# Loading the first four blocks of a linear-attention kernel as two spans of 256 tokens, two tokens per partition, and running them on quarter tiles

## The chip, the cores and the metric

One core of one Trainium2 chip. The metric is the device time of one execution in microseconds (us), from the first to the last event on the core. The profile's own span is some 2 us shorter than this time. The median of the kernel before was 227.73 us when the prediction was made (3 runs, 227.59 to 228.28).

## The reference

Linear attention with a decay per head over 4 sequences of 768 tokens, 8 heads of 64, then a feed-forward part with a gate `h * cos(h)` over all 3,072 tokens. Inputs and output are float32.

```
for b in range(nb):                       # blocks of 64 tokens, in order
    intra = einsum('bhic,bhjc->bhij', qb, kb) * Dmask
    intra = einsum('bhij,bhjd->bhid', intra, vb)
    inter = einsum('bhid,bhde->bhie', qb * lam_pow, kv_state)
    out[:, :, sl] = intra + inter
    kv_state = lam_block * kv_state + einsum('bhsd,bhse->bhde', kb_dec, vb)
...
x = out.transpose(0, 2, 1, 3).reshape(3072, 512)
h = x @ w_in                              # 512 -> 2048
return (h * cos(h)) @ w_out               # 2048 -> 512
```

## The kernel before

The kernel works on blocks of 128 tokens, 24 in all, and on 7 feed-forward tiles of 2 or 4 blocks. A small planner in the program puts all tasks in order for each engine. Some words that come back: the lead-in is the time until the first feed-forward matmul; a hidden matmul is one with `w_in`, a projection one with `w_out`; scores are the products of q and k, masked ones those after the mask; an eviction copies a finished product out of PSUM, where TensorE's rows write (the `ps_` tiles); the granted clock is the share of its full clock that TensorE was given. The parts that matter here are the loads of a block (q, k and v, each token of each head a run of 256 bytes), the chain of loads and weights, and the dummy matmuls of the lead-in.

```
def add_load(n, prio, deps=()):
    b, s0 = n // NB, (n % NB) * P
    for j, (name, src) in enumerate((("q_f", q), ("k_f", k), ("v_f", v))):
        def emit(name=name, src=src):
            t = loads.tile([P, H, D], F32, tag=name, name=name)
            i = nc.sync.dma_start(out=t, in_=src[b, :, s0:s0 + P, :].transpose([1, 0, 2]))
            # ... waits for every d in deps
...
if n >= DMA_FROM:          # from block 8 on: q and k transposed by DMA, on the queue of the loads
    first_out, T[n] = dma("SP", 1.2, 1.3, transposes_dma, n - LAG + 1.5, [a, b], get="qkT", ordered=False)
...
# ORDER = "b0 b1 b2 b3 i0 i1 i2 i3 o0 o1 o2 o3": four blocks, w_in in quarters, w_out in quarters
for at, name in enumerate(names):
    which, n = name[0], int(name[1:])
    deps = [kept[-4 if which != "b" else -2]] if at and (names[at - 1][0] == "b") != (which == "b") else []
    # weights wait for block 2's v, block 4's loads for the third quarter of w_out
...
def keep_awake(us, at, cols):            # dummies on TensorE until the first feed-forward matmul
    for _ in range(int(us / (cols / (1200.0 if at < 5.0 else 2400.0) + 0.0025))):
        nc.tensor.matmul(idle_ps[:, :cols], lhsT=ident, rhs=ident[:, :cols], start=True, stop=True)
```

## Time and profile before

| | before |
|---|---|
| time, median | 227.73 us |
| span of the profiled run, granted clock of TensorE | 226.4 us, 0.992 |
| TensorE busy | 208.4 us, 92% |
| VectorE busy | 118.6 us, 52% |
| first feed-forward matmul | 23.03 us |
| block 4's first load leaves | 38.36 us |

TensorE is the bound, so what can be won are its waits; the prediction below shows where they are. Two views are needed to follow what comes later. The first is the queue of SyncE in the timeline (start, duration, engine, line, operation), here the last load of the lead-in, block 4's first load, and the transpose of block 9, for which TensorE waits at 72.61:

```profile
14.12 0.81 SPq L201 DMA_DIRECT2D v_f<-in_v_dram  x1
...
38.36 0.37 SPq L201 DMA_DIRECT2D q_f<-in_q_dram  x1
...
66.22 2.62 SPq L271 DMA_TRANSPOSE qkT<-qk  x1
```

The second is the table of stretches: the stretch and its length, then busy us (and instructions) of TensorE, of its weight loads, of VectorE, ScalarE and GpSimd, then the granted clock, the share of DMA time and GB/s:

```profile
4.00:8.00 4.00, 1.61 (x21) 1.29 (x19) 1.32 (x3) 3.63 (x6) 0.51 (x1) 1.00 1.27 231
8.00:12.00 4.00, 4.00 (x69) 3.36 (x66) 1.82 (x4) 1.35 (x3) 2.54 (x3) 1.00 1.34 220
```

While only block loads move, the DMA share is above 1, and 231 and 220 GB/s move.

### The profile page before, as it was taken

How to read it: one execution, taken by the hardware profiler on the slowest of the kernel's cores; microseconds unless marked ns; L12 is line 12 of the kernel's file. 1: busy time of each engine (PE TensorE's matmuls, PEld its weight loads, DVE VectorE, ACT ScalarE, POOL GpSimd, SP SyncE). 2: the span in 40 equal slices, each digit the busy share in tenths (PEclk: the TensorE clock that was granted, in tenths of full speed). 3: DMA queues.
4: the chain of work that ended last, by engine and by line, in shares of the span. 5: the costliest groups of instructions: out<-in, count | busy, mean ns of one | idle time of the engine just before them, and what ended most of it. 6: DMA issues, size and time to landing. Idle time of an engine off the chain costs nothing.

```text
span 226.4 us, 4556 instructions
## 1 busy us (share of the span) xinstructions
PE 208.4 (92%) x1806; PEld 113.7 (50%) x1832; DVE 118.6 (52%) x210; ACT 105.4 (47%) x179; POOL 67.4 (30%) x84
## 2 busy tenths in 40 slices
PE   4899998599984999999999999999999999999993
PEld 4778443255663554454545444554545444565541
DVE  1455486047755477778766537746646343432310
ACT  5455675112462455745544454454454544544420
POOL 2469300378543474544354104412000000000000
PEclk9999999999999799999999999999999999999999
DMA  5999999999999999999999985723011001111112
GB/s 122 222 199 163 179 204 206 227 203 258 229 247 227 209 226 195 240 230 189 252 170 262 185 190 101 151 76 84 10 49 46 14 35 46 46 46 49 46 46 93
DMA packets 99764, 33.85 MB, mean 149 GB/s; under 512 B 92448, under 2 KB 96800, under 8 KB 99744
## 3 DMA queue, kind: packets, MB, share of 16 engines
q1 hardware_dynamic: 95376, 29.24, 63.0%
q0 software_dynamic: 4224, 4.19, 11.5%
q8 instruction: 14, 0.23, 0.4%
q10 hardware_dynamic: 144, 0.13, 0.2%
q14 instruction: 6, 0.05, 0.1%
HBM read 27.27 MB, written 6.29 MB: 148 GB/s over the span
## 4 chain that ended last, share of the span: by engine, by line
PE 84%; DMA 7%; ACT 4%; issue 2%; DVE 2%; POOL 0%; POOLq 0%
PE ps_h L393 35%; PE ps_f L431 33%; PE ps_s L295 4%; DMA qkT<-qk 3%; PE ps_o L320 3%; PE ps_o L324 2%; PE ps_h L489 2%; PE ps_f L393 2%; DMA q_f<-in_q_dram 2%; PE ps_t L265 2%; DMA lam_bc<-in_lam_dram 1%; PE ps_kv L308 1%; DMA out_dram<-o_sb 1%; DVE g L406 1%; ACT cos L400 1%
## 5 line engine op out<-in xcount | busy, mean ns | idle before, releaser
L400 ACT ACTIVATE cos<-ps_h,halfpi 128x512 f32<-128x512 f32 (+1 forms) x107 | 66.2, 624 | 77.3 <-PE ps_h L393 77.2
L406 DVE TENSOR_TENSOR g<-ps_h,cos 128x512 bf16<-128x512 f32 (+1 forms) x107 | 65.0, 610 | 69.9 <-ACT cos L400 69.2
L431 PE MATMUL ps_f<-w_out_sb,g 128*128 128x512 bf16 x349 | 90.6, 382 | 3.6 <-issue 1.4
L393 PE MATMUL ps_h<-xT,w_in_sb 128*128 128x512 bf16 (+1 forms) x421 | 92.5, 350 | 0.9 <-DVE g L406 0.6
L393 PEld LDWEIGHTS <-w_in_sb 128*128 128x128 bf16 x448 | 43.5, 99 | 44.0 <-issue 2.0
L431 PEld LDWEIGHTS <-g 128*128 128x128 bf16 x384 | 36.5, 98 | 41.3 <-issue 2.6
L239 POOL TENSOR_TENSOR qk<-q_f,q_scale 128x512 bf16<-128x512 f32 x23 | 24.0, 1044 | 60.3 <-DMA q_f<-in_q_dram 25.2
L302 DVE TENSOR_TENSOR s_m<-ps_s,mask 128x512 bf16<-128x512 f32 x48 | 31.2, 685 | 7.7 <-PE ps_s L295 6.3
L247 POOL TENSOR_TENSOR v_s<-v_f,v_scale 128x512 bf16<-128x512 f32 x24 | 25.1, 1044 | 24.1 <-DMA v_f<-in_v_dram 16.0
L444 ACT COPY o_sb<-ps_f 128x512 f32<-128x512 f32 x23 | 13.5, 587 | 23.8 <-PE ps_f L431 23.6
L330 ACT CAST xT<-ps_o 128x512 bf16<-128x512 f32 x24 | 13.9, 580 | 3.9 <-PE ps_o L324 3.8
L314 DVE CAST kv_bd<-ps_kv 64x256 bf16<-64x256 f32 x32 | 13.4, 418 | 2.9 <-PE ps_kv L308 2.4
L489 PE MATMUL ps_h<-ident 128*128 128x64 bf16 x232 | 12.0, 213 | 1.6 <-POOL ident masks.py:199 1.6
L295 PE MATMUL ps_s<-qkT 64*128 64x128 bf16 x192 | 9.7, 222 | 3.5 <-DMA qkT<-qk 2.8
L243 POOL CAST qk<-k_f 128x512 bf16<-128x512 f32 x20 | 12.2, 611 | 1.9 <-DMA k_f<-in_k_dram 1.7
L268 DVE COPY qkT<-ps_t 128x512 bf16<-128x512 bf16 (+1 forms) x12 | 6.1, 513 | 12.4 <-PE ps_t L265 12.2
L489 PEld LDWEIGHTS <-ident 128*128 128x128 bf16 x232 | 10.2, 111 | 2.4 <-POOL ident masks.py:199 1.6
L265 PE MATMUL ps_t<-ident,qk 128*128 128x128 bf16 x64 | 6.6, 236 | 4.4 <-DVE qk L239 2.0
L324 PE MATMUL ps_o<-s_m,v_s 128*64 128x128 bf16 x192 | 9.6, 220 | 0.0
L320 PEld LDWEIGHTS <-kv_bd 128*64 128x64 bf16 x160 | 5.1, 109 | 7.0 <-issue 5.9
L320 PE MATMUL ps_o<-qkT,kv_bd 128*64 128x128 bf16 x160 | 8.3, 225 | 0.0
L295 PEld LDWEIGHTS <-qkT 64*128 64x128 bf16 x192 | 5.5, 95 | 5.3 <-DMA qkT<-qk 3.0
(34 smaller groups left out, 58.1 us busy)
## 6 DMA issues: line engine op xcount, KB each, us to landing
q_f<-in_q_dram SPq DMA_DIRECT2D x24, 256.0 KB, 4.3
k_f<-in_k_dram SPq DMA_DIRECT2D x24, 256.0 KB, 4.7
v_f<-in_v_dram SPq DMA_DIRECT2D x24, 256.0 KB, 4.8
out_dram<-o_sb SPq DMA_DIRECT2D x23, 256.0 KB, 2.2
w_in_sb<-in_moe_w_in_dram POOLq DMA_DIRECT2D x4, 512.0 KB, 7.4
w_out_sb<-in_moe_w_out_dram POOLq DMA_DIRECT2D x4, 512.0 KB, 14.3
qkT<-qk SPq DMA_TRANSPOSE x16, 4.2
out_dram<-o_sb SPq DMA_DIRECT2D x1, 128.0 KB, 1.7
```

Source lines behind the costliest of these rows:

```text
L239: (nc.vector if n == 0 else nc.gpsimd).tensor_mul(live["qk", n][:, 0], live.pop(("q_f", n)), q_scale[:, c, :].unsqueeze(2).to_broadcast([P ...
L247: nc.gpsimd.tensor_mul(live["v_s", n], live.pop(("v_f", n)), v_scale[:, c, :].unsqueeze(2).to_broadcast([P, H, D]))
L295: nc.tensor.matmul(t[:, i, p, :], lhsT=live["qkT", n][h, 1, p, :], rhs=live["qkT", n][h, 0, p, :], start=True, stop=True)
L302: nc.vector.tensor_mul(live["s_m", n][:, i], live["s", n][:, i], mask.unsqueeze(1).to_broadcast([P, NP, P]))
L320: nc.tensor.matmul(t[h, p, :], lhsT=kv_bd[(n - 1) % NK][:, p, h], rhs=live["qkT", n][:, 0, p, :], start=(p == 0), stop=False, skip_group_c ...
L324: nc.tensor.matmul(t[h, p, :], lhsT=live["v_s", n][:, 2 * p + i, :], rhs=live["s_m", n][:, i, p, :], start=(p == 0 and c == 0), stop=True, ...
L330: nc.scalar.copy(live["xT", i][:, :, j * P:(j + 1) * P], live.pop(("o", n)))
L393: ins = nc.tensor.matmul(t[:, :cols], lhsT=w_in_sb[:, kd, f * P:(f + 1) * P], rhs=live["xT", i][:, kd, :cols], start=(kd == 0), stop=(kd = ...
L400: nc.scalar.activation(c[:, :cols], live["h", i, f][:, :cols], AF.Sin, bias=halfpi)
L406: nc.vector.tensor_mul(live["g", i][:, f, :cols], live.pop(("h", i, f))[:, :cols], live.pop(("c", i, f))[:, :cols])
L431: nc.tensor.matmul(live["f", i, j], lhsT=live["g", i][:, f, j * P:(j + 1) * P], rhs=w_out_sb[:, f, :], start=(f == 0), stop=(f == KF - 1))
L489: nc.tensor.matmul(idle_ps[:, :cols], lhsT=ident, rhs=ident[:, :cols], start=True, stop=True)
```

## The change

The intent is to shorten the lead-in. Blocks 0 to 3 become two spans of 256 tokens. Partition u holds the tokens 2u and 2u+1, which lie next to each other in memory, so a run is 512 bytes. Scores and values are then computed on 64x64 quarters of the array (64*64 in TensorE's rows), for even and odd tokens apart, with a mask that knows the order of tokens. The weights wait for k of span 1 in place of block 2's v. Their order relative to block 4's load does not change: the latter still waits for the third quarter of w_out.

```diff
-ORDER = "b0 b1 b2 b3 i0 i1 i2 i3 o0 o1 o2 o3"
+ORDER = "i0 i1 i2 i3 o0 o1 o2 o3"
+    def add_span_load(name, src, x, prio):
+        def emit():
+            t = live[name, "sp", x] = consts.tile([P, H, 2, D], F32, name=f"{name}_sp{x}")
+            return start_load(t.rearrange("u h s d -> u h (s d)"),
+                              src[0, :, 2 * P * x:2 * P * (x + 1), :].rearrange("h (u s) d -> u h (s d)", s=2), ())
+        _, load_t[name, "sp", x] = dma("SP", 1.8, 0.5, emit, prio)
...
+        def scores(hp):                       # in add_span; values() is built the same way
+            for p in range(2):
+                for s in range(2):
+                    for rows, _ in chunks:
+                        for i, h in enumerate(halves):
+                            nc.tensor.matmul(L["s", hp][i][rows, p, s, :], lhsT=L["kT"][h, s, 2 * hp + p, rows],
+                                             rhs=L["qT"][h, :, 2 * hp + p, rows], ...)
...
+                if n0 + j < 2 * SPANS:        # a block of a span is stored in two halves
+                    for s, h in enumerate(halves):
+                        nc.sync.dma_start(out=out[r0 + s:r0 + P:2, cols], in_=live["o_sb", i, j][h, cols])
+                    return
...
+    for j, (name, x) in enumerate((("q", 0), ("k", 0), ("q", 1), ("k", 1), ("v", 0), ("v", 1))):
+        add_span_load(name + "_f", {"q": q, "k": k, "v": v}[name], x, -20 + j)
+        kept.append(load_t[name + "_f", "sp", x])
+    hold = kept[-3]
-        deps = [kept[-4 if which != "b" else -2]] if at and ...
+        deps = [kept[-2]] if at and ...
-            keep_awake((t.start - now) * (0.95 if now < 2.0 else 0.6), now, D)
+            keep_awake((t.start - now) * (0.95 if now < 2.0 else 0.75), now, D)
```

Not in this excerpt: the scaling, transposes and evictions of the spans, shared between VectorE, ScalarE and GpSimd; a third buffer for the state; the planner's start times for the set-up work.

More of the change, by code (lines that the diff above doesn't have):

```diff
@@ L16 @@
 DMA_FROM = 8
+SPANS = 2
 LAG = 2
@@ L35 @@
 class Planner:
-    LAT = {"PE": 0.2, "ACT": 0.06, "DVE": 0.08, "POOL": 0.1, "SP": 0.0, "DMA": 0.0}
+    LAT = {"PE": 0.2, "ACT": 0.06, "DVE": 0.08, "POOL": 0.1, "SP": 0.0, "DMA": 0.0, "SETUP": 0.0}
+    SETUP = {"POOL": 5.6, "DVE": 5.6, "ACT": 7.5, "SP": 1.3}
     def __init__(self, bufs):
@@ L49, in order @@
     def order(self):
-        free, done = {}, []
+        free, done = dict(self.SETUP), []
         got = {tag: [] for tag in self.bufs}
@@ L137 @@
     make_identity(nc, ident)
+    pos_sp = consts.tile([P, SPANS, 2], F32)
+    nc.gpsimd.iota(pos_sp, pattern=[[2 * P, SPANS], [1, 2]], base=-S // 2, channel_multiplier=2,
+                   allow_small_or_imprecise_dtypes=True)
+    mask_sp = consts.tile([P, 2, P], F32)
+    nc.gpsimd.memset(mask_sp, 1.0)
+    for i in range(2):
+        m = mask_sp[i * D:(i + 1) * D].rearrange("u k (s t) -> u k s t", s=2)
+        nc.gpsimd.affine_select(out=m, in_=m, compare_op=ALU.is_ge, fill=0.0,
+                                base=0, pattern=[[-1, 2], [1, 2], [2, D]], channel_multiplier=-2)
     mask = consts.tile([P, P], F32)
@@ L143 @@
     nc.vector.memset(halfpi, math.pi / 2.0)
-    NK = 2
+    NK = 3
     kv_bd = [consts.tile([P, NP, P], BF16, name=f"kv_bd{i}") for i in range(NK)]
@@ L149 @@
     nc.scalar.activation(lnl, lam_bc, AF.Ln)
+    expo_sp = consts.tile([P, SPANS, H, 2], F32)
+    nc.vector.tensor_mul(expo_sp, pos_sp.unsqueeze(2).to_broadcast([P, SPANS, H, 2]),
+                         lnl.unsqueeze(1).unsqueeze(3).to_broadcast([P, SPANS, H, 2]))
+    q_sp = consts.tile([P, SPANS, H, 2], F32)
+    nc.scalar.activation(q_sp, expo_sp, AF.Exp)
     expo = consts.tile([P, NB, H], F32)
@@ L152 @@
                          lnl.unsqueeze(1).to_broadcast([P, NB, H]))
+    v_sp = consts.tile([P, SPANS, H, 2], F32)
+    nc.scalar.activation(v_sp, expo_sp, AF.Exp, scale=-1.0)
     q_scale = consts.tile([P, NB, H], F32)
@@ L194, in dma, with start_load @@
         return t, d
+    def start_load(o, x, deps):
+        i = nc.sync.dma_start(out=o, in_=x)
+        for d in deps:
+            tc.add_manual_dep(i.ins, getattr(d, "issue", d).ins.ins.name, mybir.DependencyInfo(
+                mybir.DependencyClass.Sync, mybir.DependencyReason.DATA), reason="order of loads")
+        return i
+    def add_span_load(name, src, x, prio):
[4 more added lines that the diff above has]
+        _, load_t[name, "sp", x] = dma("SP", 1.8, 0.5, emit, prio)
     def add_load(n, prio, deps=()):
@@ L200, in emit @@
                 t = loads.tile([P, H, D], F32, tag=name, name=name)
-                i = nc.sync.dma_start(out=t, in_=src[b, :, s0:s0 + P, :].transpose([1, 0, 2]))
-                for d in deps:
-                    tc.add_manual_dep(i.ins, getattr(d, "issue", d).ins.ins.name, mybir.DependencyInfo(
-                        mybir.DependencyClass.Sync, mybir.DependencyReason.DATA), reason="order of loads")
                 live[name, n] = t
-                return i
+                return start_load(t, src[b, :, s0:s0 + P, :].transpose([1, 0, 2]), deps)
             issue, load_t[name, n] = dma("SP", 1.2, 0.45, emit, prio + 0.1 * j, deps, get=name)
@@ L227 @@
     T, Sc, So, V, Vo, U, Uo = ({} for _ in range(7))
-    parts = {}
+    parts, Uo_sp = {}, {}
+    chunks = [(halves[c], c) for c in range(2)]
     def add_attention(n):
@@ L379, in add_attention, with add_span, prep, prep_k @@
             parts[n] = finish
+    def add_span(x):
+        pa = lambda part: -1000.0 + 2 * x + part
+        pv = lambda part: -990.0 + 2 * x + part
+        cut = [slice(4 * hp, 4 * hp + 4) for hp in range(2)]
+        us = {"DVE": 0.69, "POOL": 1.1}
+        vec = {"DVE": nc.vector, "POOL": nc.gpsimd}
+        L = {name: consts.tile([P, 2, H, D], BF16, name=f"{name}_sp{x}") for name in ("q", "k", "v")}
+        L.update({name: consts.tile([P, 2, NP, P], BF16, name=f"{name}_sp{x}") for name in ("qT", "kT")})
+        L["s_m"] = consts.tile([P, 2, NP, 2, P], BF16, name=f"s_m_sp{x}")
+        place = lambda t, hp: t[:, :, cut[hp]].rearrange("u s h d -> u h s d")
+        def prep(name, hp, e):
+            vec[e].tensor_mul(place(L[name], hp), live[name + "_f", "sp", x][:, cut[hp]],
+                              (q_sp if name == "q" else v_sp)[:, x, cut[hp]].unsqueeze(3).to_broadcast([P, 4, 2, D]))
+        def prep_k(hp):
+            nc.scalar.copy(place(L["k"], hp), live["k_f", "sp", x][:, cut[hp]])
+        def transposes(name, hp):
+            t = L["t", name, hp] = bank(("ps_t", "ps_f")[hp], [P, 2, 2, P], BF16)
+            for s in range(2):
+                for p in range(2):
+                    h = 4 * hp + 2 * p
+                    nc.tensor.transpose(t[:, s, p, :], L[name[0]][:, s, h:h + 2, :], ident)
+        def transposes_out(name, hp, e):
+            (nc.scalar.copy if e == "ACT" else nc.vector.tensor_copy)(L[name][:, :, 2 * hp:2 * hp + 2, :], L["t", name, hp])
+        def scores_bank():
+            L["s", 1] = [bank("ps_t" if x else "ps_o", [P, 2, 2, P], F32)]
+        def scores(hp):
+            if x and hp:
+                L["s", 1].append(bank("ps_f", [P, 2, 2, P], F32))
+            elif hp:
+                live["spare"] = bank("ps_h", [P, NP, P], F32)
+                L["s", 1].append(live["spare"].rearrange("u (p s) t -> u p s t", p=2))
+            else:
+                t = bank("ps_s", [P, 2, 2, 2, P], F32)
+                L["s", hp] = [t[:, 0], t[:, 1]]
+            for p in range(2):
+                for s in range(2):
+                    for rows, _ in chunks:
+                        for i, h in enumerate(halves):
+                            nc.tensor.matmul(L["s", hp][i][rows, p, s, :], lhsT=L["kT"][h, s, 2 * hp + p, rows],
+                                             rhs=L["qT"][h, :, 2 * hp + p, rows],
+                                             start=True, stop=True, skip_group_check=True)
+        def scores_out(hp, i):
+            nc.vector.tensor_mul(L["s_m"][:, i, 2 * hp:2 * hp + 2], L["s", hp][i],
+                                 mask_sp.unsqueeze(1).to_broadcast([P, 2, 2, P]))
+        def update(rows, n):
+            for p in range(NP):
+                for s in range(2):
+                    for i, h in enumerate(halves):
+                        nc.tensor.matmul(kv_ps[h, p, :], lhsT=L["k"][rows, s, 2 * p + i, :], rhs=L["v"][rows, s, 2 * p + i, :],
+                                         start=(n == 0 and p == 0 and s == 0), stop=True, skip_group_check=True)
+        def update_out(n, h, e):
+            (nc.scalar.copy if e == "ACT" else nc.vector.tensor_copy)(kv_bd[n % NK][h, :, h], kv_ps[h])
+        def values_bank():
+            if not x:
+                L["o"] = [bank("ps_o", [P, NP, P], F32), live["spare"]]
+        def values():
+            if x:
+                t = bank("ps_s", [P, 2, NP, P], F32)
+                L["o"] = [t[:, 0], t[:, 1]]
+            for p in range(NP):
+                for s in range(2):
+                    for rows, c in chunks:
+                        for i, h in enumerate(halves):
+                            nc.tensor.matmul(L["o"][c][h, p, :], lhsT=L["v"][rows, s, 2 * p + i, :],
+                                             rhs=L["s_m"][rows, i, p, s, :],
+                                             start=(p == 0 and s == 0), stop=True, skip_group_check=True)
+        def carried(c):
+            for p in range(NP):
+                nc.tensor.matmul(L["o"][c][:, p, :].rearrange("e (s u) -> e s u", s=2),
+                                 lhsT=kv_bd[(2 * x + c - 1) % NK][:, p, :], rhs=L["qT"][:, :, p, chunks[c][0]],
+                                 start=False, stop=True, skip_group_check=True)
+        def values_out(c, e, pairs):
+            if ("xT", 0) not in live:
+                live["xT", 0] = work.tile([P, KD, 4 * P], BF16, tag="xT", name="xT")
+            n = 2 * x + c
+            (nc.scalar.copy if e == "ACT" else nc.vector.tensor_copy)(
+                live["xT", 0][:, pairs, n * P:(n + 1) * P], L["o"][c][:, pairs])
+        so, kt, v_t = [], [], []
+        for hp in range(2):
+            e = "DVE" if hp == 0 else "POOL"
+            a = pl.add(e, us[e], [load_t["q_f", "sp", x]], partial(prep, "q", hp, e), pa(-0.9 + 0.1 * hp))
+            kt.append(pl.add("ACT", 0.61, [load_t["k_f", "sp", x]], partial(prep_k, hp), pa(-0.9 + 0.1 * hp)))
+            e = "DVE" if hp == 0 else "POOL"
+            v_t.append(pl.add(e, us[e], [load_t["v_f", "sp", x]], partial(prep, "v", hp, e), pa(-0.7 + 0.1 * hp)))
+            outs = []
+            for name, src in (("qT", a), ("kT", kt[hp])):
+                e = "ACT" if x else "DVE"
+                t = pl.add("PE", MM(P, 4), [src], partial(transposes, name, hp), pa(-0.5 + 0.1 * hp), get=("ps_t", "ps_f")[hp])
+                outs.append(pl.add(e, 0.58 if e == "ACT" else 0.42, [t], partial(transposes_out, name, hp, e), pa(-0.5 + 0.1 * hp)))
+                t.frees = [outs[-1]]
+            if hp:
+                s0 = pl.add("PE", 0.0, outs, scores_bank, pa(0.1 + 0.1 * hp), get="ps_t" if x else "ps_o")
+                s1 = pl.add("PE", MM(P, 8) + 0.2, [s0], partial(scores, hp), pa(0.1 + 0.1 * hp), get="ps_f" if x else None)
+            else:
+                s0 = None
+                s1 = pl.add("PE", MM(P, 8) + 0.2, outs, partial(scores, hp), pa(0.1 + 0.1 * hp), get="ps_s")
+            two = [pl.add("DVE", 0.69, [s1], partial(scores_out, hp, i), pa(0.1 + 0.1 * hp + 0.05 * i)) for i in range(2)]
+            s1.frees = two
+            if s0:
+                s0.frees = two
+            so += two
+        c0, c1 = 2 * x, 2 * x + 1
+        out_of = {}
+        def add_update(c):
+            n = 2 * x + c
+            U[n] = pl.add("PE", MM(D, 16) + 0.2, v_t + kt + Uo_sp.get(n - 1, []), partial(update, chunks[c][0], n), n - 1100.0 if n < 3 else -900.0)
+            Uo_sp[n] = [pl.add(e, 0.4, [U[n]] + ([V[n - NK + 1]] if n > NK - 1 else []), partial(update_out, n, h, e), n - 1100.0 if n < 3 else -900.0)
+                        for h, e in zip(halves, ("ACT", "DVE"))]
+        add_update(0)
+        v0 = pl.add("PE", 0.0, so + v_t, values_bank, pv(0.2), get=None if x else "ps_o")
+        v1 = pl.add("PE", MM(P, 8) + 0.2, [v0], values, pv(0.2), get="ps_s" if x else None)
+        first_out = pl.add("PE", MM(P, 4), [v1] + Uo_sp[c0 - 1], partial(carried, 0), pv(0.25)) if x else v1
+        second = pl.add("PE", MM(P, 4), [v1] + Uo_sp[c0], partial(carried, 1), pv(0.3))
+        V[c0], V[c1] = first_out, second
+        Vo[c0] = pl.add("ACT", 0.6, [first_out], partial(values_out, 0, "ACT", slice(0, NP)), pv(0.3))
+        ends = [pl.add(e, 0.4, [second], partial(values_out, 1, e, p), pv(0.35))
+                for e, p in (("DVE", slice(0, 2)), ("ACT", slice(2, NP)))]
+        v0.frees = v1.frees = [Vo[c0]] + ends
+        Vo[c1] = pl.add("SETUP", 0.0, ends, None, 0.0, lat=0.15)
+        add_update(1)
+        Uo[c1] = pl.add("SETUP", 0.0, Uo_sp[c1], None, 0.0, lat=0.1)
@@ L464, in add_ffn @@
             evacs[0].frees = stores
+    kept = []
+    for j, (name, x) in enumerate((("q", 0), ("k", 0), ("q", 1), ("k", 1), ("v", 0), ("v", 1))):
+        add_span_load(name + "_f", {"q": q, "k": k, "v": v}[name], x, -20 + j)
+        kept.append(load_t[name + "_f", "sp", x])
     names = ORDER.split()
-    names += [f"b{n}" for n in range(NBLK) if f"b{n}" not in names]
-    kept = []
+    names += [f"b{n}" for n in range(2 * SPANS, NBLK) if f"b{n}" not in names]
+    hold = kept[-3]
     for at, name in enumerate(names):
         which, n = name[0], int(name[1:])
-        deps = [kept[-4 if which != "b" else -2]] if at and (names[at - 1][0] == "b") != (which == "b") else []
+        deps = [kept[-2]] if at and (names[at - 1][0] == "b") != (which == "b") else []
         if which == "b":
@@ L478 @@
         hold = deps[0] if deps else (None if which == "b" else hold)
+    for x in range(SPANS):
+        add_span(x)
     for i in range(len(TILES)):
-        for n in range(first[i] + (i > 0), min(first[i + 1] + 1, NBLK)):
+        for n in range(max(2 * SPANS, first[i] + (i > 0)), min(first[i + 1] + 1, NBLK)):
             add_attention(n)
```

## The prediction

> **What bounds the kernel now.** I read the page first, then the timeline of the lead-in, the timeline of TensorE alone, and the busy time by stretches. The page says that TensorE is busy 92% of the span, so only its waits can be won back:
>
> ```profile
> span 226.4 us, 4556 instructions
> PE 208.4 (92%) x1806; PEld 113.7 (50%) x1832; DVE 118.6 (52%) x210; ACT 105.4 (47%) x179; POOL 67.4 (30%) x84
> PEclk9999999999999799999999999999999999999999
> ```
>
> Part of this busy time is line 489, dummy matmuls[...] while the first four blocks come in. So the lead-in must be read from its own timeline:
>
> ```profile
> 7.49 1.04 POOL L247 TENSOR_TENSOR v_s<-v_f,v_scale 128x512 bf16<-128x512 f32 x1 [5.42 <-DMA v_f<-in_v_dram]
> 11.03 1.04 POOL L247 TENSOR_TENSOR v_s<-v_f,v_scale 128x512 bf16<-128x512 f32 x1 [1.38 <-DMA v_f<-in_v_dram]
> 15.29 1.04 POOL L247 TENSOR_TENSOR v_s<-v_f,v_scale 128x512 bf16<-128x512 f32 x1 [2.04 <-DMA v_f<-in_v_dram]
> 16.28 0.94 POOL L216 DMA_DIRECT2D w_in_sb<-in_moe_w_in_dram  x1
> ...
> 22.39 0.59 ACT L330 CAST xT<-ps_o 128x512 bf16<-128x512 f32 x1 [0.70 <-PE ps_o L324]
> ...
> 23.03 1.89 PE L393 MATMUL ps_h<-xT,w_in_sb 128*128 128x512 bf16 x7
> ```
>
> The third load of each block lands at 7.49, 11.03 and 15.29 us: 3.90 us per block of 768 KB (786,432 bytes), or 202 GB/s. The lead-in is paced by these loads, the weights' first transfer waits for them until 16.28, and the useful work of the feed-forward part starts at 23.03.
>
> TensorE's own timeline shows two later stalls:
>
> ```profile
> 37.64 2.75 PE L431 MATMUL ps_f<-w_out_sb,g 128*128 128x512 bf16 x12 [0.64 <-DVE g L406]
> 40.89 1.02 PE L431 MATMUL ps_f<-w_out_sb,g 128*128 128x512 bf16 x4 [0.50 <-DMA w_out_sb<-in_moe_w_out_dram]
> 43.87 0.40 PE L265 MATMUL ps_t<-ident,qk 128*128 128x128 bf16 x4 [1.96 <-POOL qk L239]
> ...
> 72.61 0.40 PE L295 MATMUL ps_s<-qkT 64*128 64x128 bf16 x8 [2.85 <-DMA qkT<-qk]
> ```
>
> The first is 0.64 + 0.50 + 1.96 = 3.10 us. Behind the 1.96 stands a DMA: block 4's q load is issued only at 38.36, when the third quarter of the output weights has landed. The second is 2.85 us for a DMA transpose, and costs more than it shows, as the stretch after it ran at 0.53 of the clock:
>
> ```profile
> 33.00:37.00 4.00, 3.95 (x18) 1.70 (x18) 3.14 (x6) 3.16 (x5) 0.00 (x0) 1.00 1.24 207
> ...
> 73.00:76.00 3.00, 3.00 (x14) 1.64 (x13) 2.12 (x4) 0.95 (x2) 2.23 (x3) 0.53 1.02 187
> 76.00:80.00 4.00, 3.74 (x46) 2.20 (x46) 1.27 (x4) 2.06 (x4) 0.77 (x2) 0.93 1.14 218
> ```
>
> Lost clock: 3.00 x 0.47 + 4.00 x 0.07 = 1.7 us. The rest of the span is TensorE at work, apart from a tail of some 6 us that the change doesn't touch. The last two figures of a row are the DMA share and GB/s: 207 while only weights move, counted in bf16 although float32 is read, so about 400 GB/s of reads. The same engines thus read twice as fast in 2 KB runs as in the 256 bytes of a block load's descriptors.
>
> [...] the trace has 0.69 us for each masked 128x512 eviction, while eight matmuls take 0.40. [...]
>
> **The change part by part.**
>
> Loads. Twelve loads of 1,024 descriptors of 256 bytes become six of 1,024 with 512 bytes. One load took 1.30 us. At unchanged time per descriptor a span load takes 1.3 us[...]. I take 1.7 (308 GB/s)[...], as the weights show the engines can read at 400. The first q load of before was in by about 5.0, so q0, k0, q1, k1, v0, v1 land at about 5.4, 7.1, 8.8, 10.5, 12.2, 13.9, against some 19 for before's last.
>
> Compute of the lead-in. It does not shrink with the loads. VectorE of before: one scaling 0.69, eight transpose copies 0.43, eight masked scores 0.645 = 9.3 us. After, from the program's order: four scalings 2.76, four copies 1.7, eight masked scores 5.2, four state halves at 0.43 = 1.7, two output halves at 0.42 = 0.8: 12.2 us. It starts at 5.5 (the scale's activation ends there), so cannot end before 17.7. By hand, engine by engine in program order:
> - ScalarE is free for k at about 7.4 (two more small activations than before); k halves at 8.0 and 8.6; VectorE has the first kT at about 9.4, scales q1 until 10.1, second kT 10.5.
> - Masked scores of span 0 until 13.2, v0's scaling 13.9; ScalarE's transposes of span 1 give scores at 14.2, masked by 15.6.
> - Then a strict chain of states, each update waiting for the eviction before it, halves one after the other on ScalarE and VectorE: about 16.3, 18.4, 20.0. Span 1's second scores and v1's scaling fill VectorE between.
> - Carried product 20.3, then three evictions in a row, 0.6 + 0.42 + 0.38: 21.7. With some overlap that I could not settle, 20.3 to 21.7; I take **21.0, a gain of 2.0 us**. Quarter tiles add 64 small matmuls to scores and values[...] in place of dummies: nothing.
>
> Weights. Their first transfer now waits for k1 (10.5), not for block 2's v (15.29, issued 16.28). From there v0 and v1 have still some 3.4 us of traffic, the weights 4.19 MB / 0.205 = 20.5 us. Last landing: 9.2 + 3.4 + 20.5 + 1.5 (latency) = 34.6, third quarter 2.5 earlier, about **32.1 against 38.36: 6 us earlier**.
>
> First stall. Hidden matmuls take 14.0 us: 35.0; wait for the last gate 0.64; sixteen projections 3.46: 39.1. Block 4's loads leave at 32.1, its q lands 4.25 later, scaling and k's copy 1.75: 38.1. So the waits of 0.50 and 1.96 both go: **2.46 us**; I count 2.2.
>
> Second stall. The transpose is issued behind 21 loads and four stores from block 4 on, and before, stores ready at 42.5 left only at 51.79: that queue is paced by the DMA, not by TensorE. It comes some 6 us earlier, less about 0.5 for stores split in two; TensorE only 4.2. So the 2.85 shrinks by about 1.3, and with a shorter pause part of the lost clock comes back. I count **1.8 of 4.5 us**.
>
> Against: the planner has reordered everything after, which I put at 0.3. Sum 2.0 + 2.2 + 1.8 - 0.3 = 5.7: 227.7 - 5.7 = **222.0 us**.
>
> **The rivals.**
> 1. The gain stays at the lead-in. VectorE's chain takes the place of the loads, and the later stalls move along with it, since the queue's stores and in-order waits tie both together. For: VectorE's 12.2 us and the serial evictions. Against: block 4's loads wait only for weights. It would make 224.5 to 226.
> 2. 512-byte descriptors hardly help[...]: 224 to 225.[...]
> 3. All stalls vanish, clock loss included: 2.0 + 2.5 + 4.5 = 9.0, or 218.7. For: DMA comes further forward than TensorE. Against: the transposes share the queue with loads that keep it full until about 130 us.
> 4. Slower: a late order of the chain, weights taking bandwidth from v1. I find no path to more than 3 us of loss.
>
> **Range and chances.** The 2% mark is 223.2. The centre lies 1.2 below; I give rivals 1 and 2 together about a third. Range 218.8 to 225.8; faster 0.68, same 0.29, slower 0.03.
>
> **What would show it.** Right: span loads about 1.7 us apart; first hidden matmul at 20 to 22 with VectorE nearly gapless from 9 us on and state evictions ahead of the last xT; block 4's first load at 31 to 33.5; no wait for w_out or POOL after the first projection; a shorter wait for the DMA transpose around 65 us. Wrong: the first hidden matmul after 22.3, a wait on v_f late in the lead-in, block 4's first load later than 35, or a new half-clock stretch.

## The result, and the profile after

| | before | after |
|---|---|---|
| time, median (runs) | 228.0 us (4, 227.59 to 229.32) | 221.26 us (4, 220.45 to 221.9) |
| ratio of fast runs | | 0.9693, 95% interval 0.9641 to 0.9745: faster |
| span of the profiled run | 226.4 us | 219.6 us |
| first feed-forward matmul | 23.03 | 21.42 |
| first projection (behind the 0.64 us wait) | 37.64 | 36.38 |
| block 1's projection resumes | 44.10 | 40.66 |
| block 4's first load leaves | 38.36 | 32.19 |

A ratio here is the mean time of one kernel's fast runs over that of the other's of the same rounds, so it is not quite the ratio of the medians. The page's first lines of the kernel after:

```profile
span 219.6 us, 4682 instructions
PE 207.1 (94%) x1885; PEld 112.2 (51%) x1885; DVE 122.6 (56%) x217; ACT 105.5 (48%) x181; POOL 65.8 (30%) x85
```

TensorE's busy time, dummies included, is nearly the same, 1.3 us less by the page, and its share rises since the span shrinks: waits were won back. The lead-in on GpSimd, from its timeline (the bracket is the idle time before and what ended it):

```profile
5.62 1.54 POOL L427 TENSOR_TENSOR q_sp<-q_f_sp,q_sp 128x512 bf16<-128x512 f32 x1 [2.11 <-ACT q_sp L166]
8.51 1.04 POOL L427 TENSOR_TENSOR q_sp<-q_f_sp,q_sp 128x512 bf16<-128x512 f32 x1 [1.35 <-DMA q_f_sp<-in_q_dram]
10.24 1.68 POOL L246 DMA_DIRECT2D w_in_sb<-in_moe_w_in_dram  x2 [0.69 <-DMA k_f_sp<-in_k_dram]
12.66 1.04 POOL L427 TENSOR_TENSOR v_sp<-v_f_sp,v_sp 128x512 bf16<-128x512 f32 x1 [0.74 <-DMA v_f_sp<-in_v_dram]
```

With the times to landing of the same trace, q1, k1, v0 and v1 landed at about 8.4, 10.0, 12.6 and 14.0 us, and the weights left at 10.24 where they left at 16.28. Two rows of VectorE, for the scalings of which GpSimd does the other half:

```profile
9.06 1.03 DVE L427 TENSOR_TENSOR q_sp<-q_f_sp,q_sp 128x512 bf16<-128x512 f32 x1
12.74 1.50 DVE L427 TENSOR_TENSOR v_sp<-v_f_sp,v_sp 128x512 bf16<-128x512 f32 x1
```

The two stretches shown for the kernel before now carry half as much again (346 and 344 GB/s):

```profile
4.00:8.00 4.00, 3.03 (x72) 2.79 (x70) 1.78 (x5) 3.95 (x9) 1.54 (x1) 1.00 1.15 346
8.00:12.00 4.00, 3.58 (x98) 3.01 (x95) 3.36 (x7) 1.88 (x4) 2.72 (x3) 1.00 1.15 344
12.00:16.00 4.00, 2.95 (x120) 2.60 (x119) 3.94 (x7) 2.76 (x6) 3.32 (x4) 1.00 1.17 199
...
18.00:20.00 2.00, 1.94 (x57) 1.62 (x56) 1.29 (x3) 0.36 (x1) 1.24 (x2) 0.68 1.25 208
20.00:22.00 2.00, 2.00 (x34) 1.48 (x32) 0.85 (x2) 1.09 (x3) 0.00 (x0) 0.50 1.24 206
```

The row from 12 us shows VectorE, the third busy figure, at work 3.94 of 4.00 us: it has taken the place of the loads as the pace of the lead-in (number 3 below, with more work on VectorE, bears this out). The last two rows show the granted clock at 0.68 and 0.50. TensorE's timeline and the queue of SyncE:

```profile
18.06 0.19 PE L671 MATMUL ps_h<-ident 128*128 128x64 bf16 x1 [0.95 <-issue]
...
21.42 2.24 PE L565 MATMUL ps_h<-xT,w_in_sb 128*128 128x512 bf16 x8
...
36.38 3.61 PE L603 MATMUL ps_f<-w_out_sb,g 128*128 128x512 bf16 x16 [0.64 <-DVE g L578]
39.83 0.61 PE L296 MATMUL ps_t<-ident,qk 128*128 128x128 bf16 x8
40.66 1.02 PE L603 MATMUL ps_f<-w_out_sb,g 128*128 128x512 bf16 x4 [0.23 <-ACT o_sb L616]
...
65.94 0.40 PE L326 MATMUL ps_s<-qkT 64*128 64x128 bf16 x8 [0.77 <-DMA qkT<-qk]
```

```profile
32.19 0.37 SPq L216 DMA_DIRECT2D q_f<-in_q_dram  x1
...
60.29 1.45 SPq L623 DMA_DIRECT2D out_dram<-o_sb  x2
61.90 2.01 SPq L302 DMA_TRANSPOSE qkT<-qk  x1
```

The waits for w_out and for block 4 are gone: sixteen projections and eight transposes run on from 36.38. The wait for the transposed block 9 is 0.77 where it was 2.85, and no half clock follows it.

The gain can be followed along the span by the start of the same work: 1.61 us at the first feed-forward matmul, 1.26 at the first projection, 3.44 at block 1's projection, 6.67 at block 9's scores. The eviction that ScalarE starts at 91.61 us before starts at 85.19 after, which is 6.42, and the last one at 223.01 and 216.58 us, which is 6.43. So **the whole gain is made before 85 us**, and after that both kernels run in step. (The planner put some pieces in another order: at 40.66 us the kernel after had done four more transposes than the kernel before at 44.10. So these shifts are good to a few tenths.) The rest of the 6.8 us between the spans is in the last store.

### The profile page after: what moved, and what is told of

The parts are those of the page before. It is cut to its first block, busy times and chain, and to the rows that moved or that the text cites. A ratio compares the mean times of both kernels' runs of the same rounds, so it can differ in the third digit from the quotient of the medians.

```text
span 219.6 us, 4682 instructions
## 1 busy us (share of the span) xinstructions
PE 207.1 (94%) x1885; PEld 112.2 (51%) x1885; DVE 122.6 (56%) x217; ACT 105.5 (48%) x181; POOL 65.8 (30%) x85
## 4 chain that ended last, share of the span: by engine, by line
PE 83%; DMA 5%; DVE 3%; SPq 3%; ACT 2%; issue 2%; POOL 1%; POOLq 0%
PE ps_f L603 36%; PE ps_h L565 34%; PE ps_s L326 3%; DMA qkT<-qk 2%; PE ps_o L351 2%; SPq L216 2%; PE ps_f L565 2%; PE ps_o L355 2%; DVE s_m_sp L464 2%; DMA lam_bc<-in_lam_dram 1%; SPq L302 1%; PE ps_h L671 1%; DMA out_dram<-o_sb 1%; PE ps_kv L339 1%; ACT o_sb L616 1%
## 5 line engine op out<-in xcount | busy, mean ns | idle before, releaser
L603 PE MATMUL ps_f<-w_out_sb,g 128*128 128x512 bf16 x368 | 92.3, 379 | 0.9 <-DVE g L578 0.6
L270 POOL TENSOR_TENSOR qk<-q_f,q_scale 128x512 bf16<-128x512 f32 x20 | 20.8, 1042 | 61.0 <-PE ps_kv L339 21.8
L333 DVE TENSOR_TENSOR s_m<-ps_s,mask 128x512 bf16<-128x512 f32 x40 | 26.1, 686 | 3.6 <-PE ps_s L326 3.2
L278 POOL TENSOR_TENSOR v_s<-v_f,v_scale 128x512 bf16<-128x512 f32 x20 | 20.8, 1042 | 14.0 <-issue 5.4
L345 DVE CAST kv_bd<-ps_kv 64x256 bf16<-64x256 f32 x32 | 13.4, 417 | 1.7 <-PE ps_kv L339 1.3
L274 POOL CAST qk<-k_f 128x512 bf16<-128x512 f32 x20 | 12.2, 610 | 1.3 <-DMA k_f<-in_k_dram 1.3
L361 ACT CAST xT<-ps_o 128x512 bf16<-128x512 f32 x20 | 11.6, 579 | 2.0 <-PE ps_o L355 1.8
L671 PE MATMUL ps_h<-ident 128*128 128x64 bf16 x201 | 9.9, 212 | 2.6 <-POOL ident masks.py:199 1.6
L326 PE MATMUL ps_s<-qkT 64*128 64x128 bf16 x160 | 7.9, 219 | 1.8 <-DMA qkT<-qk 1.8
L355 PE MATMUL ps_o<-s_m,v_s 128*64 128x128 bf16 x160 | 7.9, 220 | 0.0
L355 PEld LDWEIGHTS <-v_s 128*64 128x64 bf16 x160 | 5.6, 110 | 1.3 <-issue 1.3
L299 DVE COPY qkT<-ps_t 128x1024 bf16<-128x1024 bf16 x4 | 2.8, 691 | 5.2 <-PE ps_t L296 5.2
```

The lines of the kernel that those rows point to most:

```text
L270: (nc.vector if n == 0 else nc.gpsimd).tensor_mul(live["qk", n][:, 0], live.pop(("q_f", n)), q_scale[:, c, :].unsqueeze(2).to_broadcast([P ...
L278: nc.gpsimd.tensor_mul(live["v_s", n], live.pop(("v_f", n)), v_scale[:, c, :].unsqueeze(2).to_broadcast([P, H, D]))
L326: nc.tensor.matmul(t[:, i, p, :], lhsT=live["qkT", n][h, 1, p, :], rhs=live["qkT", n][h, 0, p, :], start=True, stop=True)
L333: nc.vector.tensor_mul(live["s_m", n][:, i], live["s", n][:, i], mask.unsqueeze(1).to_broadcast([P, NP, P]))
L355: nc.tensor.matmul(t[h, p, :], lhsT=live["v_s", n][:, 2 * p + i, :], rhs=live["s_m", n][:, i, p, :], start=(p == 0 and c == 0), stop=True, ...
L603: nc.tensor.matmul(live["f", i, j], lhsT=live["g", i][:, f, j * P:(j + 1) * P], rhs=w_out_sb[:, f, :], start=(f == 0), stop=(f == KF - 1))
```

## The experiments

Theory A says that two chains race: TensorE's, from the lead-in on, and that of the transfers, from block 4's first load through the shared queue to the transposes. The lead-in gives some 1.3 us and the transfers the rest, because they leave 6 us earlier. The rivals: the lead-in's compute or the layout gives it all, the earlier place of the weights gives it all and could have been had without the change, or TensorE's half clock sets the size.

The experiments ran on three chips (that of the result above is not on record), where the kernel before took 229.38 us (numbers 1 to 4), 228.51 (5 to 8) and 229.8 (9 to 12) in the same rounds. So ratios to before are compared, and a difference in us from the kernel after is worked out from them.

### 1 and 2: block 4's load later and earlier

One edit moves the wait of block 4's first load by one quarter of w_out, and nothing else; the order of the program stays the same.

```diff
-                return start_load(t, src[b, :, s0:s0 + P, :].transpose([1, 0, 2]), deps)
+                return start_load(t, src[b, :, s0:s0 + P, :].transpose([1, 0, 2]), real or deps)
-            add_load(n, at, deps)
+            add_load(n, at, deps, [kept[-1]] if deps else None)      # later: w_out's fourth quarter
+            add_load(n, at, deps, [kept[-3]] if deps else None)      # earlier, in the second kernel: its second
```

> Only one wait is changed: block 4's first load waits for the last quarter of the output weights in place of the third, some 2.5 us later; program order on every engine is the same. Theory A (in the changed kernel the end is set by the DMA chain from block 4's loads to the transposes of blocks 9 to 11): the transposes come 2.5 us later, their waits on TensorE grow by that much, the total is up by 1.8 to 2.5 us (about 223.4). Theory B (the lead-in sets the end, and later waits just move along): block 4's transposed q and k are ready 0.9 us after TensorE needs them, the rest is absorbed: up by 0 to 0.9 us.

> The same wait moved the other way: block 4's first load waits for the second quarter of the output weights, some 2.5 us earlier; program order the same. Theory A1 (that chain is paced by the bytes and descriptors that the 16 engines must move): the loads take their time from the weights, the last weights land later, blocks 9 to 11 come at nearly the same time: total within 0.5 us. Theory A2 (it is paced by when the queue starts): the waits of 0.77, 0.18 and 0.84 us vanish and the total falls by 1 to 2 us. Theory B (lead-in): no change.

Later: 226.75 us median (223.63 to 227.52, the longest labelled slow), ratio to before 0.9839, 0.9764 to 0.9915. That is 1.5% or 3.3 us on the kernel after, more than theory A's 1.8 to 2.5, with a wide spread: the three fast runs took 223.63, 226.64 and 226.87. Earlier: 222.5 us (222.15 to 222.7), ratio 0.9698, 0.9673 to 0.9722, the same as the kernel after. TensorE in the late one, and last a row of its queue:

```profile
35.66 3.61 PE L603 MATMUL ps_f<-w_out_sb,g 128*128 128x512 bf16 x16 [0.64 <-DVE g L578]
...
69.07 0.61 PE L326 MATMUL ps_s<-qkT 64*128 64x128 bf16 x8 [3.51 <-DMA qkT<-qk]
...
66.24 1.32 SPq L302 DMA_TRANSPOSE qkT<-qk  x1
```

Its lead-in was even 0.7 us better than that of the kernel after. With block 4's load at 35.39 in place of 32.19, block 9's transpose left at 66.24, as late as before's 66.22, and TensorE stood 3.51 us at it; the clock of 68 to 72 us was 0.60. So about half of the gain hangs on this load alone. The early kernel sent the load at 29.99 us, but its transposes left no earlier (56.91 and 62.58 against 56.51 and 61.90). Two reasons are at hand, not told apart: the loads now shared the engines with the weights, and the queue has stores in it that wait for TensorE, which in this trace had lost clock in the lead-in (0.56 from 20 to 22 us; first projection at 37.29). An earlier load than in the kernel after is worth nothing here.

### 3: a longer lead-in

Three extra multiplications of 0.69 us on VectorE ahead of span 1's last values.

```diff
+        def pad():
+            for _ in range(3):
+                nc.vector.tensor_mul(padding, <a 128x512 part of q_f>, <the same of k_f>)
         def values_bank():
+            if x:
+                pad()
```

> Three multiplications of 128x512 (0.69 us each) with an unused result are put into VectorE's order just ahead of the third state's eviction, on the serial chain at the end of the lead-in: the first hidden matmul moves from 21.4 to about 23.5, the loads and weights stay. Theory A (DMA chain sets the end): the waits for transposes (0.77, 0.18, 0.84) take up most of it, total up by 0.3 to 1.0 us. Theory B (lead-in sets the end): up by 2.1 us.

223.97 us (223.3 to 225.7), ratio 0.9775, 0.9727 to 0.9823: 0.8% or 1.9 us on the kernel after, 1.5 us (medians) on the early-load kernel of the same rounds. Neither theory's number came out pure. The 2.1 us of work on VectorE moved the first feed-forward matmul by 1.74, to 23.16. The profiled run is the slowest of the four, and lost clock besides (0.50 from 24 to 26 us), so that its first projection came at 39.38, 3.0 later. Block 4's load left at 32.65, nearly as before the edit, but block 9's transpose came 1.9 us later, as the queue shows:

```profile
62.15 1.45 SPq L631 DMA_DIRECT2D out_dram<-o_sb  x2
63.77 1.33 SPq L303 DMA_TRANSPOSE qkT<-qk  x1
```

The two stores of the first tile in front of it left 1.9 us later too (62.15 against 60.29); ScalarE began their eviction at 60.78 against 57.78, after a later TensorE. Loads of the same queue waited as well, for buffers that GpSimd had still to read (2.2 us once). Which of these waits carries the delay is not shown, but the two chains are tied: a later TensorE makes the queue later too. The theory as first put, with the transfers independent of TensorE, falls.

### 4 to 6: the width of the runs against the place of the weights

Number 4 keeps everything but the runs: each span load becomes two transfers with runs of 256 bytes. Number 5 keeps 512 bytes and lets the weights wait for v of span 1. Number 6 does both.

```diff
# 4 and 6
-            return start_load(t.rearrange("u h s d -> u h (s d)"), src[...].rearrange("h (u s) d -> u h (s d)", s=2), ())
+            for s in range(2):
+                i = start_load(t[:, :, s, :], src[...].rearrange("h (u s) d -> u h s d", s=2)[:, :, s, :], ())
+            return i
# 5 and 6
-    hold = kept[-3]
+    hold = kept[-1]
```

> Each span load is made of two, one for each token of the pair, so that the descriptors are 256 bytes as before while layout, arithmetic and order stay. If the descriptor's size makes the loads' speed (the step of the prediction that put a span load at 1.7 us, and found 512 bytes nearly as dear as 256): the twelve transfers take about 1.3 us each, k1 lands near 13, v1 near 19, the weights and block 4's loads come 4 to 5.5 us later, and the total is up by 4 to 6 us, to 225.5 to 227.5, most of the gain undone. If the larger descriptors hardly matter and the gain is of the layout and the weights' earlier place: up by less than 1 us.

> The changed kernel, but the weights wait for the last span load (v1) in place of k1, so they and the span loads no longer share the engines; the planner may reorder. Partner of the next run. v1 lands at about 13.7, the first weights leave at about 15, near the 16.28 of the kernel before; the first hidden matmul waits for them until about 21.5 to 22.5; block 4's first load leaves at about 36. If the weights' earlier place is worth what the prediction gave it (most of the 2.46 us of the first stall and part of the second), the total is 3 to 5 us above the changed kernel, 225 to 227 here. If the lead-in alone sets the end: within 1 us.

> The same, with the span loads made of 256-byte descriptors (two transfers for each). With no weights beside them the descriptor's size stands alone. Size matters: 3.15 MB at 230 to 250 GB/s end at about 17 in place of 13.7, weights, lead-in and block 4 come 3 to 3.5 us later than in the run before, total up by 3 to 3.5 us on it. Size hardly matters: within 1 us of it. If the starving of v1 by the weights was most of what the run with 256 bytes and early weights lost (9 us), this one is faster than that.

| | runs of | weights leave | time, median (range) | ratio to before |
|---|---|---|---|---|
| after | 512 | 10.24 | 221.26 (220.45 to 221.9) | 0.9693 |
| 4 | 256 | 12.39 | 231.4 (227.93 to 231.6) | 1.0092, 1.0064 to 1.0121 |
| 5 | 512 | 15.42 | 227.08 (225.16 to 227.29) | 0.9899, 0.9835 to 0.9963 |
| 6 | 256 | 19.70 | 230.51 (229.41 to 231.53) | 1.0085, 1.0053 to 1.0117 |

Of the five runs of number 4, three (231.4 to 231.6) are labelled slow, and the reported ratio is what those three give; the other two, 230.23 and 227.93, come to 0.9986. It is 3 to 4% slower than the kernel after either way, slower than both theories had it, and not told apart from number 6.

Read with number 6 as the floor, the gain comes apart. The layout with quarter tiles alone, with 256-byte runs and weights that leave later than before's 16.28, costs 0.85% or 1.9 us. The width alone gives 1.9% (6 to 5, 4.3 us); the weights, which wait for v of span 1 in both, leave 4.28 us earlier with it. The earlier weights on top give 2.1% (5 to after, 4.7 us). But the earlier weights with narrow runs (6 to 4) give nothing that these runs show: what the starving below cost number 4 is about what the later weights cost number 6. A row of number 4's stretches, and one of VectorE's timeline, show why:

```profile
8.00:12.00 4.00, 2.60 (x75) 2.16 (x75) 1.87 (x5) 1.33 (x3) 1.34 (x1) 1.00 1.03 232
```

```profile
24.51 0.69 DVE L429 TENSOR_TENSOR v_sp<-v_f_sp,v_sp 128x512 bf16<-128x512 f32 x1 [7.45 <-DMA v_f_sp<-in_v_dram]
```

Split into 256 bytes, the same loads move at 232 GB/s where the wide ones moved at 344, and the last one is sent at 12.2 us in place of 6.9. Numbers 4 and 6 halve the runs and double the number of transfers at once. The traces also hold one record for each packet that a DMA engine moved: one of 512 bytes took 27.0 ns on average (kernel after, 8 to 10 us), one of 256 bytes 18.1 (number 4, 8 to 12 us). So the wide packets carry 1.34 times the bytes in the same time of an engine, and the rest of the 1.48 (344 to 232) goes with the share of DMA time, 1.15 against 1.03; that part could be the number of transfers. The last transfer of v1, sent at 12.2 us, took 12.2 us to land, where the median of its four was 4.2. In the kernel after, v0 and v1 took 7.1 us each with the weights beside them, and in number 5 with no weights before 15.42 they took 7.1 and 7.2. So the wide loads, all sent by 8.4 us, lost nothing to the weights, and the narrow one, sent with the weights, was starved by them; in number 6, without weights beside it, none of the four took more than 5.8 us.

Number 5 also confirms how the weights' place pays. It brings the first stall back:

```profile
39.98 1.02 PE L603 MATMUL ps_f<-w_out_sb,g 128*128 128x512 bf16 x4 [1.51 <-DMA w_out_sb<-in_moe_w_out_dram]
```

Its first feed-forward matmul came at 21.09 us, no later than in the kernel after: an early end of the lead-in without early weights was worth 1.0%, or 2.3 us.

### 7 and 8: the clock at the end of the lead-in

In the profiled run of the kernel after, the clock fell to half at 18.7 us, until 22.1. Number 7 puts 25 more dummies ahead of the third state update. Number 8 does this and gives span 1's two outputs banks of their own, so that VectorE's half need not wait for ScalarE's eviction of the other, as it did for 1.41 us at 20.89 in the kernel after.

```diff
         def update(rows, n):
+            for _ in range(25 if n == 2 else 0):
+                nc.tensor.matmul(idle_ps[:, :D], lhsT=ident, rhs=ident[:, :D], start=True, stop=True)
# 8 as well
-            if not x:
-                L["o"] = [bank("ps_o", [P, NP, P], F32), live["spare"]]
+            L["o"] = [bank("ps_o", ...), live["spare"] if not x else bank("ps_h", ...)]
```

> 25 dummy matmuls are added ahead of the third state update, where TensorE idled for 0.95 us and the clock then fell to half[...]; nothing else changes. If the half clock at the end of the lead-in costs what the trace of the changed kernel says (hidden matmuls gain only 1.25 us where the first one had gained 1.6) and the lead-in carries through to the end: clock 1.0 in that stretch, total down by 0.4 to 0.9 us on the changed kernel. If later waits take it up: no change.

> As the run before, and span 1's two output halves go to PSUM tiles of their own, so that VectorE's half no longer waits for ScalarE's eviction of the other block (the profile had 1.41 us of wait there, of which some 0.5 is on the path). If the lead-in carries through: another 0.3 to 0.7 us down. If the later transposes set the end: no change on the run before.

Number 7: 221.07 us (220.68 to 222.47), ratio 0.9674, 0.9624 to 0.9724. Number 8: 221.76 us (220.76 to 225.09, the longest slow), ratio 0.9678, 0.9621 to 0.9736. Both are the same as the kernel after, and both edits failed at what they were to do in the profiled run: TensorE still stood 1.14 and 1.15 us at 18 us. Number 7 then fell to half clock (its first eight hidden matmuls took 3.31 us, against 1.89 in the control; granted clock 0.984 over the span); number 8 kept its clock (0.999), but its first feed-forward matmul came at 22.03. What the profile of number 8 shows is worth more than its time:

```profile
37.88 2.75 PE L601 MATMUL ps_f<-w_out_sb,g 128*128 128x512 bf16 x12 [0.64 <-DVE g L576]
...
61.43 1.32 SPq L302 DMA_TRANSPOSE qkT<-qk  x1
```

The first row is of TensorE, the second of the queue: the first projection at 37.88, later than before's 37.64, in a span of 219.3 us, and with no wait for a transposed block. Block 4's load left at 32.37 and block 9's transpose at 61.43. So in this run **7 us were won with TensorE's chain no earlier than before at that point**; only the transfers were. Number 7, with its first projection at 38.97, shows the same in a span of 220.8 us. Number 8 and the control (number 12) kept their clock in the lead-in, and their profiled runs took 221.02 and 223.16 us, against 221.34 in the kernel after: no gain from keeping it is seen, so the third rival finds no support.

### 9: earlier weights in the kernel before

```diff
-        deps = [kept[-4 if which != "b" else -2]] if at and ...
+        deps = [kept[-7 if which != "b" else -2]] if at and ...      # weights wait for block 1's v
```

> The kernel before with one change: the weights' first transfer and block 4's first load follow the same chain, but the weights no longer wait for block 2's v load, they wait for block 1's (11.0 us in place of 15.3). It asks whether the kernel before could have had the earlier weights without the wide loads. Theory W (the wide loads are what makes the earlier weights affordable; loads of 256 bytes lose to the weights' long runs): block 3's loads land several us late (19 to 23 us instead of 18.5), the first hidden matmul comes at 25 to 28, and the time is the same as before or up to 3 us longer, 227.5 to 231. Theory R (the order of the loads is the whole gain, the width does nothing): first hidden matmul at about 23, third quarter of the output weights some 4 us earlier, time 223 to 225.

233.73 us (233.24 to 234.01), ratio 1.0174, 1.0127 to 1.022: 4.0 us slower than before, and slower than theory W had it (227.5 to 231). The mechanism is W's:

```profile
11.97 0.94 POOL L216 DMA_DIRECT2D w_in_sb<-in_moe_w_in_dram  x1
...
28.77 1.04 POOL L247 TENSOR_TENSOR v_s<-v_f,v_scale 128x512 bf16<-128x512 f32 x1 [9.99 <-DMA v_f<-in_v_dram]
```

Block 3's v, sent at 13.81 us, landed 14.8 us later, and the first feed-forward matmul came at 33.45. This earlier place of the weights is not a gain that the kernel before had left lying.

### 10 to 12: fewer DMA transposes, and a control

`DMA_FROM = 10` and `DMA_FROM = 12` transpose blocks 8 and 9, or 8 to 11, on TensorE. Number 12 is the kernel after, unedited, on the same chip.

> The kernel after, with blocks 8 and 9 transposed on TensorE and not by DMA. Two transposes on TensorE and their waits cost about 0.44 us of TensorE each (a row of the trace: eight matmuls with 128 rows in 0.40), 0.9 us together; the waits for transposed blocks at 65.9 and 71.3 (0.77 and 0.18 us) go, and the queue has two transposes fewer. Theory A (the transposes no longer hold anything up after the change, TensorE's work is the end): +0.0 to +1.0 us, 221 to 222.5. Theory Q (the queue with loads, transposes and stores still paces the middle): -0.5 to -1.5 us, 219.5 to 220.7.

> As the last one with blocks 8 to 11 on TensorE: 1.8 us more of TensorE work against waits of 0.77, 0.18 and 0.84 = 1.79. Theory A: +0.0 to +1.5 us. Theory Q: -0.5 to -2 us. If waits for transposed blocks appear at block 12 in their place, the queue is only pushed along.

> The changed kernel once more, unedited, on the chip of the three others, as their control: 220.4 to 222.0 us, ratio to before 0.966 to 0.972.

| | time, median (range) | ratio to before |
|---|---|---|
| 10: from block 10 | 222.37 (222.02 to 222.72) | 0.9681, 0.9637 to 0.9726 |
| 11: from block 12 | 223.08 (222.26 to 224.33) | 0.9717, 0.9664 to 0.977 |
| 12: control | 222.52 (221.68 to 225.17, the longest slow) | 0.9676, 0.9617 to 0.9734 |

The waits for transposed blocks were gone from the profiles of 10 and 11 up to 90 us, and no time was won, as theory A had it. Its reason, that TensorE pays in work what it saves in waits, is not shown: a gain may hide, as both profiled runs lost clock in the lead-in (0.50 from 20 to 24 us) and had the first projection at 38.45 and 38.49, against 36.20 in the control. The control is the more telling run; its median lies a little above the expected 222.0, its ratio within what was expected. It is the same program as the kernel after, and its profile differs in just the places in dispute:

```profile
18.58 0.19 PE L671 MATMUL ps_h<-ident 128*128 128x64 bf16 x1 [1.56 <-issue]
...
67.23 0.40 PE L326 MATMUL ps_s<-qkT 64*128 64x128 bf16 x8 [2.23 <-DMA qkT<-qk]
```

```profile
20.00:22.00 2.00, 1.66 (x35) 1.21 (x36) 0.86 (x3) 0.96 (x2) 0.13 (x1) 1.00 1.25 207
...
70.00:74.00 4.00, 4.00 (x46) 2.44 (x44) 1.12 (x3) 1.63 (x4) 1.16 (x2) 0.69 1.09 199
```

It kept its clock through the lead-in, and its first projection came at 36.20. Its transpose of block 9 left 0.65 us later than in the other run (62.55), TensorE stood 2.23 us in place of 0.77, and the clock of 70 to 74 us fell to 0.69. Its span was 221.5, against 219.6. The difference arises right there: ScalarE's evictions come 0.18 us earlier than in the other run at 57.60, and 1.82 later from 87.01 on. **One program thus shows both ends**, some 2 us apart, with 0.65 us between them in the queue. Why the transpose left later is not shown; it may be another chip, too.

## Why the prediction was right

It said 222.0, with 218.8 to 225.8, and faster by over 2%. It came to 221.26, and 222.52 in the control. By its own steps:

- **Loads at 1.7 us each: right.** The trace before had no load in runs of 512 bytes; the 1.7 was an estimate of the author's, above the 1.30 us measured for a load in runs of 256. Expected landings of q1, k1, v0 and v1 were 8.8, 10.5, 12.2 and 13.9, found 8.4, 10.0, 12.6 and 14.0. The choice of 308 GB/s was on the low side: 344 to 346 was found.
- **VectorE takes over in the lead-in: right, its sum 1.2 us short.** The rows of its timeline add up to 13.4 us, not 12.2. The difference is in the four scalings: two took 0.69 each as counted, the other two 1.03 and 1.50, while GpSimd scaled the other half of the same span. In the trace the engine that started second was the slow one: where GpSimd had started first (12.66 against 12.74, and 8.51 against 9.06), it took 1.04 and VectorE 1.50 and 1.03; where VectorE had (5.57 against 5.62), it took 0.69 and GpSimd 1.54, not 1.04. The fourth pair did not overlap (14.48 and 15.93), and took 1.06 and 0.69. What holds the second one up is not shown. The lead-in's end at 21.0 was found at 21.42.
- **A gain of 2.0 in the lead-in: too high.** It was 1.61 at the first feed-forward matmul, and 1.26 once the half clock of 18 to 22 us was paid. The prediction named a new half-clock stretch as a thing that would prove it wrong, and one came, but it was short, and only in some runs.
- **Block 4's load at 32.1: right**, at 32.19. Its sum starts at 9.2 us, which the prediction does not derive; from its own landing of k1, 10.5, it would have given 33.4. Its 1.5 for latency is an estimate of the author's too; the nearest to it in the trace is a lone store of 128 KB, 1.7 us from issue to landing. So the hit has some luck in it. **2.2 for the first stall: right.** The shift between both kernels grew from 1.26 to 3.44 us, so 2.18.
- **1.8 for the second stall less 0.3 for the planner, so 1.5: too low.** The shift grew from 3.44 to 6.42 us, so 2.98. Here a size failed, and part of the reason: "that queue is paced by the DMA, not by TensorE". The transpose was to come about 5.5 us earlier and came 4.32 earlier (61.90 against 66.22), since the queue ahead of it waits for TensorE in part; number 3 shows that a later TensorE delays it. The shorter wait came from elsewhere as well: from leaving to the scores it took 4.0 us in this run, 6.4 in before's. Why a transpose took 6.4, 4.7 (control) or 2.8 us (number 1) is not settled. The 1.7 us of lost clock after before's wait went, but three waits came up in the kernel after in their place (0.73, 0.18 and 0.84 us, at 68 to 76 us).
- **The sum: luck in part.** It came within 0.7 us since a lead-in 0.7 too high stood against a second stall 1.5 too low.
- **Rival 1**, that the gain stays at the lead-in, falls with numbers 1 and 8. **Rival 2** falls with the rate of 344 GB/s and with numbers 4 to 6: width is worth 4.3 us with late weights, and makes the earlier weights affordable; its 224 to 225 was an estimate of the author's that no run shows. **Rival 3**, 218.7, was not reached: the best run, with a granted clock of 1.000, took 220.45.

One step was right for a narrower reason than the prediction gave. It let the weights go earlier and v0 and v1 lose nothing by it. That holds since all wide loads had been sent before. Numbers 4 and 9 show what happens otherwise; the prediction named it under its fourth rival ("weights taking bandwidth from v1") and had no term for it. Whether the length of a run or being sent ahead of the weights protects the loads is not told apart by these runs, because the wide loads have both.

## What to carry to other kernels

When a load is made wider, look beyond the stage that it feeds: here 1.3 of 6.4 us were there at the first projection (number 5, with an early lead-in and late weights, won 2.3), and most came from transfers further down the chain that could leave 6 us earlier. Check whether an early start of a large transfer meets small ones still to be sent: such a move was worth 4.7 us behind wide loads (number 5 to the kernel after), cost 4.0 us among narrow ones in number 9, and gave nothing in number 4. Where a kernel has two chains of about the same length, look at a second profile of the same program before explaining a difference of a per cent by an edit.

## What these runs leave open

- **The cost of a short run.** The stretches show 220 to 231 GB/s before and 344 to 346 after, 1.5 times. In time for a packet, the records show 27.0 ns for 512 bytes against 18.1 for 256 in number 4, 1.49 times, and against 24.9 before (8 to 12 us), 1.08 times. Why 256 bytes took 24.9 ns in one kernel and 18.1 in the other is not shown, nor whether runs wider than 512 bytes would load faster still: the weights, in runs of 2 KB, were read at about 400 GB/s (an estimate: twice the 199 to 207 counted).
- **Short runs beside the weights.** 256 KB with runs of 256 bytes took 14.8 us to land beside the weights in number 9 and 12.2 in number 4, where the medians were 5.1 (number 9's twelve lead-in loads) and 4.2 (number 4's four of v). The runs show what it costs, not how it comes about.
- **When the clock falls.** It fell to half after gaps of 0.95 us (kernel after) and 1.14 (number 7) at 18 us, and not after 1.56 in the control, the same program as the first, nor after 1.15 in number 8; a stall of 2.23 us at 67 us in the control was followed by 0.69 from 70 to 74, and in number 4, where TensorE did nothing from 20 to 24 us, the clock was 0.50 from 24 to 32. The length of one gap doesn't tell it in these runs.
- **The time of a DMA transpose beside loads.** From its leaving to its use 2.8 to 6.4 us passed in these runs.
